# First x of a fused attention and MoE kernel by casting loads on GpSimd's queue, transposed head by head, with the first weight chunk in halves

## The chip, the cores and the metric

The kernel runs on one core of one Trainium2 chip. The metric is the device time of one execution in microseconds (us), lower is better. The core has five engines with programs of their own: PE (TensorE, matrix products; its weight loads are listed as PEld), DVE (VectorE), ACT (ScalarE), POOL (GpSimd) and SP (SyncE, here only a queue for transfers). They meet through semaphores. Sixteen DMA engines carry the transfers that SP, ACT and POOL issue.

## The reference

```python
# x: (B 8, H 8, S 512, D 64)   state: (8, 8, Ns 32, 64)   scale = 1/8
a      = softmax(scale * x @ state^T)          # (B,H,512,32)
xread  = a @ state                             # (B,H,512,64)
a2     = softmax(scale * state @ x^T)          # (B,H,32,512)
sread  = a2 @ x                                # (B,H,32,64)
t      = concat([xread, sread], axis=2)        # (B,H,544,64)
t      = t.transpose(0,2,1,3).reshape(4352, 512)
h      = t @ w_in                              # 512 -> 2048
out    = (h / (1 + exp(-h))) @ w_out           # silu, 2048 -> 512
```

Inputs and output are fp32; the kernel computes in bf16 with fp32 sums.

## The kernel before, in words

**Tiling.** The 512 features are four groups `kt` of 128 (two heads, `half` 0 and 1, of 64 each). The 512 rows of a batch are four groups `c` of 128, row 4p+c on partition p. The kernel goes batch by batch. `xread @ w_in` is not computed through xread: the state of a batch is first multiplied with w_in, and the result `W1` (`w1_m` on PE into two PSUM banks, `w1_e` to copy it out as bf16) has 256 rows (8 heads x 32 states), so that `h = a @ W1` (`g1`, two matmuls of 128x512 and a silu on ACT) and `out = g @ w_out` (`G2(b, ft)`: four matmuls, one for each row group `tt`; `ft` counts sixteen groups of 128 of the 2048 features).

**One batch's attention.** x arrives as fp32 (`load_x`), is cast to bf16 into `x_n` (`cast_x`; its rows have a column of ones on either side, for the sums of sread), transposed on PE (`x_T`, four 128x128 transposes for one kt) and copied out of PSUM into `xT` (`x_Te`). `st_T` transposes the state and writes the two halves of `sbd`. `sc` computes the scores of one kt (four matmuls), `ex` exponentiates them on ACT into `en`, `norm_s` sums and inverts on DVE, `norm_m` multiplies into `an`, and `a_T` transposes `an` on PE and copies it into `aT`, which g1 reads. `sread_m`, `sread_n` and `sread_t` compute sread from `en` and `x_n`.

**Order.** The order of instructions is written out by hand (`manual_schedule`): each engine executes its own in the order of the program. Transfers are in order within the issuing engine too: an engine that waits holds up the transfers written behind the wait. A load that POOL issues takes one of eight semaphores in turn, and the ninth waits until the first of them is done. For batch 0 (lines 327 to 412): SP issues four loads of x (one kt each, line 91), ACT issues the state (line 327), POOL builds the identity, casts the state, and issues the first w_in chunk (512 of 2048 columns), the first w_out chunk (four ft), the state of batch 1 and the second w_in chunk. All w loads cast fp32 to bf16 in the transfer. PE fills its idle time with `warm` matmuls on zeros (line 320). DVE casts x (line 79 is `cp` on DVE, line 83 `cp` on ACT, line 81 on POOL); the four kt go through transposes, copies, scores and exponentials one after the other; then come the two halves of the normalization (POOL takes kt 0 and 1, DVE kt 2 and 3, line 185), the first `w1_m` and `w1_e`, `a_T`, and the first g1. After that the g1 and G2 of batch 0 are interleaved with the attention of batch 1 and the later chunks of `W1` (lines 411 to 482). From batch 1 on, `phase(k, fill)` runs the 64 matmuls of batch k's G2 and inserts the attention and g1 of the next batches at numbered steps; x is there transposed by DMA.

Of the kernel before, what the change touches and what calls it, by code (L numbers as in the profile page):

```python
# [19 lines left out]
def kernel(  # L20
# [8 lines left out]
    nc = tc.nc  # L29
# [16 lines left out]
    x_f = [pers.tile([128, KT, 2, 256], FP32, name=f"x_f{i}") for i in range(2)]  # L46
    x_n = [pers.tile([128, KT, 4, 132], BF16, name=f"x_n{i}") for i in range(2)]
    x_u = pers.tile([128, KT, 4, 2, D], BF16, name="x_u")
    xT = [pers.tile([128, KT, 4, 128], BF16, name=f"xT{i}") for i in range(2)]
# [27 lines left out]
    def cp(eng, dst, src):  # L77
        if eng == "dve":
            nc.vector.tensor_copy(dst, src)  # L79
        elif eng == "pool":  # L80
            nc.gpsimd.tensor_copy(dst, src)
        else:
            nc.scalar.activation(dst, src, func=COPY, bias=0.0)  # L83
# [5 lines left out]
    def load_x(b, eng, kt=0, n=4):  # L89
        dst = x_f[b % 2][:, ds(kt, n)].rearrange("p k h e -> p (k h) e")  # L90
        eng.dma_start(dst, x_src(b, kt, n))
# [3 lines left out]

    def load_wi(j):
        nc.gpsimd.dma_start(
            w_in_sb[:, :, ds(512 * j, 512)], win_re[:, :, ds(512 * j, 512)]
        )

    def load_wo(j):
        nc.gpsimd.dma_start(w_out_sb[:, ds(4 * j, 4), :], wout_re[:, ds(4 * j, 4), :])

# [23 lines left out]
    def x_T(b, kt, bk):  # L127
        v = bf(bk).rearrange("p (k c t) -> p k c t", k=2, c=4)
        for c in range(4):
            nc.tensor.transpose(  # L130
                v[:, kt % 2, c, :], x_n[b % 2][:, kt, c, ds(2, 128)], ident[:]
            )

    def x_Te(b, kt, n, bk, eng):
# [111 lines left out]

    def w1_m(b, j, bks):
        for kt in range(KT):
            for half in range(2):
                nc.tensor.matmul(  # L250
                    bank[bks[half]][ds(32 * kt, 32), :],
                    sbd[ds(64 * half, 64), b, kt, half, :],
                    w_in_sb[ds(64 * half, 64), kt, ds(512 * j, 512)],
                    start=True,
                    stop=True,
                    skip_group_check=True,
                    tile_position=(64 * half, 32 * kt),
                )

    def w1_e(b, j, bks, engs):  # L260
        for half in range(2):
            cp(engs[half], W1[b % 2][:, half, ds(512 * j, 512)], bank[bks[half]][:])

# [61 lines left out]
    with tc.manual_schedule():  # L325

        nc.scalar.dma_start(st0_f[:], state[0].rearrange("h ns d -> ns h d"))
        for kt in range(KT):
            load_x(0, nc.sync, kt, 1)
        nc.vector.memset(zeros[:], 0.0)  # L330
        nc.vector.memset(sbd[:], 0.0)
        for i in range(2):
            nc.vector.memset(x_n[i][:, :, :, 1:131:129], 1.0)
        make_identity(nc, ident[:])
        nc.scalar.preload_act_table(EXP)
        cp("pool", st_nat[:, 0, :], st0_f[:])
        load_wi(0)
        load_wo(0)
        load_st(1)
        load_wi(1)  # L340
        warm(28, "o0")

# [12 lines left out]
        def W1x(b, j, bks, engs):  # L355
            w1_m(b, j, bks)
            w1_e(b, j, bks, engs)

# [13 lines left out]

        cast_x(0, "dve", (0,))
        x_T(0, 0, XB[0])
        x_Te(0, 0, 1, XB[0], "act")
        cast_x(0, "dve", (1,))
        st_T(0, "a1", "act", "dve")
        cast_x(0, "dve", (2, 3))
        warm(4, "w1")
        x_T(0, 1, XB[1])  # L380
        x_Te(0, 1, 1, XB[1], "act")
        sc(0, 0, SB[0])
        ex(0, 0, 1, SB[0])
        warm(3, "w1")
        x_T(0, 2, XB[2])
        x_Te(0, 2, 1, XB[2], "act")
        sc(0, 1, SB[1])
        ex(0, 1, 1, SB[1])
        x_T(0, 3, XB[3])
        x_Te(0, 3, 1, XB[3], "dve")  # L390
        warm(2, "o0")
        for kt in (2, 3):
            sc(0, kt, SB[kt])
            ex(0, kt, 1, SB[kt])
        norm_s(0, 0, 2)
        norm_m(0, "pool", 0, 2)
        norm_s(0, 2, 2)
        norm_m(0, "dve", 2, 2)
        nc.scalar.preload_act_table(SILU)
        warm(7, "o0", 512)  # L400
        w1_m(0, 0, ("w0", "w1"))
        w1_e(0, 0, ("w0", "w1"), ("act", "act"))
        a_T(0, (("a0", "dve"), ("a1", "dve")))
        warm(2, "o0", 512)
        load_x(1, nc.gpsimd, 0, 2)
        load_x(1, nc.gpsimd, 2, 2)
        load_wo(1)
        load_wi(2)


        for ft in range(4):
            g1(0, ft)
        G2(0, 0)
        st_T(1, "a0", "dve", "dve")
        sread_m(0, "a1")
        sread_n(0, "a1")
        G2(0, 1)
        sread_t(0, "a1", "dve")
        G2(0, 2)
        W1x(0, 1, AB, DA)  # L420
# [7 lines left out]
        cast_x(1, "dve", (2,))  # L428
        load_wo(2)
        load_wi(3)  # L430
        load_wo(3)
        load_x(2, nc.gpsimd)
# [54 lines left out]
        def W1p(b, i):  # L487
            for j in range(2):
                w1_m(b, 2 * i + j, WP[j])
            for j in range(2):  # L490
                w1_e(b, 2 * i + j, WP[j], DD if j == 0 else ("act", "act"))

# [103 lines left out]
```

## Time and profile before

| | us |
|---|---|
| median of 13 runs | 223.31 |
| lowest and highest | 222.42, 226.24 |
| the profiled execution | 222.59 |
| its span (first to last instruction) | 220.8 |
| PE busy in the span | 210.2 |
| ACT busy | 133.3 |
| DVE busy | 83.6 |
| POOL busy | 40.7 |
| first g1 matmul starts | 11.77 |

How to read the profile's rows: a row of the timeline has the start, the time that the group covers, the engine and line of the code, the operation, what it writes and reads, how many instructions are merged in it, and in brackets how long the engine had been idle before, with what ended that. L79 is line 79. "x4" are four instructions. A window row has the busy time of each engine in that stretch with the instructions in brackets, then the granted clock, the mean busy share of the 16 DMA engines (over 1 where transfers overlap in an engine) and the GB/s that were written. "DMA to landing" counts from the start of the issuing instruction to the transfer's end. The loads of before that matter here: x from SP is issued at 0.74, 1.27, 1.76 and 2.29 us and lands after 2.6, 3.3, 3.5 and 3.7 us; the first w_in chunk is issued at 4.13 and lands after 5.5; the first w_out chunk at 5.06, after 7.7; the second w_in chunk at 6.49, after 9.0; the second w_out chunk at 11.67, after 10.3, and G2(0, 4), which reads it, starts at 22.01.

### The profile page before, as it was taken

What the parts mean: (1) busy time and instruction counts of PE and PEld (TensorE: products, weight loads), DVE (VectorE), ACT (ScalarE), POOL (GpSimd) and SP (SyncE); (2) the same over time, 40 slices, a digit from 0 to 9 for tenths busy, and PEclk for the clock granted to TensorE, in tenths of its full rate; (3) what the DMA queues carried; (4) which work ended last, traced back from release to release, by engine and by line L of the source; (5) the groups of instructions that cost most, each with busy time, mean ns of one, the idle gap of its engine ahead of it and who ended that gap; (6) DMA issues with size and microseconds to landing.
All of it is one profiled execution on the core that took longest, in us unless ns stands there. A gap on an engine that the chain in (4) does not pass through costs nothing.

```text
span 220.8 us, 4060 instructions
## 1 busy us (share of the span) xinstructions
PE 210.2 (95%) x1626; PEld 102.9 (47%) x1654; DVE 83.6 (38%) x162; ACT 133.3 (60%) x220; POOL 40.7 (18%) x78
## 2 busy tenths in 40 slices
PE   7799999999999999999999999999999999999993
PEld 7444433445444444444444444444453444566552
DVE  4736253526840483138412851085206701111110
ACT  3845876586568946776477837692669377433210
POOL 4634722005200052002500250025000200000000
PEclk9999999999999999999999999999999999999999
DMA  6999997292070386118540655066511311111112
GB/s 202 152 264 234 182 268 90 79 269 84 3 190 0 81 240 160 47 39 223 157 107 0 216 169 120 25 186 194 99 47 47 98 47 47 53 47 47 47 50 95
DMA packets 33988, 26.00 MB, mean 118 GB/s; under 512 B 18736, under 2 KB 29232, under 8 KB 33968
## 3 DMA queue, kind: packets, MB, share of 16 engines
q1 hardware_dynamic: 26720, 18.75, 30.2%
q0 software_dynamic: 6688, 6.52, 16.4%
q10 hardware_dynamic: 560, 0.46, 0.6%
q8 instruction: 13, 0.21, 0.4%
q14 instruction: 7, 0.06, 0.1%
HBM read 17.30 MB, written 8.91 MB: 119 GB/s over the span
## 4 chain that ended last, share of the span: by engine, by line
PE 87%; ACT 4%; DMA 3%; issue 3%; POOL 1%; DVE 1%; ACTq 0%
PE ps_o L295 44%; PE ps_h L271 25%; PE ps_w L295 4%; PE ps_h L282 3%; DMA aT<-an 3%; PE ps_o L320 2%; PE ps_a L159 2%; PE ps_w L250 2%; POOL an L185 1%; PE ps_a L250 1%; PE ps_h L250 1%; ACT W L83 1%; PE ps_a L217 1%; PE ps_a L130 1%; ACT g L279 1%
## 5 line engine op out<-in xcount | busy, mean ns | idle before, releaser
L295 PE MATMUL ps_o<-w_out_sb,g 128*128 128x512 bf16 x458 | 126.5, 379 | 2.5 <-issue 1.9
L279 ACT ACTIVATE g<-ps_h 128x512 bf16<-128x512 f32 x128 | 75.5, 598 | 51.0 <-PE ps_h L271 49.3
L271 PE MATMUL ps_h<-aT,W 128*128 128x512 bf16 x251 | 74.0, 379 | 1.1 <-ACT g L279 0.6
L295 PEld LDWEIGHTS <-g 128*128 128x128 bf16 x512 | 47.9, 98 | 52.5 <-issue 3.9
L79 DVE COPY o_sb<-ps_o 128x512 f32<-128x512 f32 x30 | 20.6, 689 | 90.7 <-PE ps_o L295 69.6
L271 PEld LDWEIGHTS <-W 128*128 128x128 bf16 x256 | 24.2, 98 | 32.1 <-DMA aT<-an 2.7
L185 POOL TENSOR_TENSOR an<-en,rs 128x512 bf16<-128x512 bf16 x7 | 10.0, 1429 | 90.6 <-ACT W L83 49.7
L141 POOL CAST x_u<-x_f 128x256 bf16<-128x256 f32 x40 | 14.2, 406 | 24.0 <-DMA x_f<-in_x_dram 24.0
L79 DVE CAST W<-ps_w 128x512 bf16<-128x512 f32 x24 | 15.4, 682 | 0.4 <-PE ps_w L250 0.3
L83 ACT ACTIVATE W<-ps_h 128x512 bf16<-128x512 f32 x24 | 13.1, 602 | 0.5 <-PE ps_h L250 0.5
L290 ACT ACTIVATE g_s<-ps_h 128x256 bf16<-128x256 f32 x16 | 6.1, 384 | 11.4 <-PE ps_h L282 11.4
L180 DVE TENSOR_REDUCE rs<-en 128x32 f32<-128x1024 bf16 (+1 forms) x9 | 9.8, 1094 | 4.1 <-ACT en L170 4.1
L170 ACT ACT_TABLE_LOAD x7 | 9.0, 1283 | 1.8 <-DVE xT L79 1.6
L282 PE MATMUL ps_h<-xsT,w_in_sb 128*128 128x256 bf16 x64 | 9.6, 273 | 0.0
L295 PE MATMUL ps_w<-w_out_sb,g 128*128 128x512 bf16 x32 | 9.5, 379 | 0.1
L170 ACT ACTIVATE en<-ps_a 128x512 bf16<-128x512 f32 (+1 forms) x16 | 8.3, 568 | 0.2
L282 PEld LDWEIGHTS <-w_in_sb 128*128 128x128 bf16 x64 | 6.3, 98 | 4.1
L506 ACT ACT_TABLE_LOAD x6 | 7.7, 1283 | 0.1
L159 PEld LDWEIGHTS <-xT 128*128 128x128 bf16 x128 | 5.9, 98 | 3.6 <-ACT xT L83 0.3
L79 DVE COPY sbd<-ps_a 64x128 bf16<-64x128 bf16 x15 | 4.3, 289 | 8.6 <-PE ps_a L119 8.2
L79 DVE CAST W<-ps_a 128x512 bf16<-128x512 f32 x6 | 4.2, 692 | 9.0 <-PE ps_a L250 9.0
L250 PEld LDWEIGHTS <-sbd 64*32 64x32 bf16 x256 | 3.1, 89 | 9.0 <-issue 8.8
(61 smaller groups left out, 129.2 us busy)
## 6 DMA issues: line engine op xcount, KB each, us to landing
out_dram<-o_sb SPq DMA_DIRECT2D x32, 256.0 KB, 2.5
x_f<-in_x_dram SPq DMA_DIRECT2D x5, 1024.0 KB, 7.0
w_in_sb<-in_moe_w_in_dram POOLq DMA_DIRECT2D x4, 512.0 KB, 8.9
w_out_sb<-in_moe_w_out_dram POOLq DMA_DIRECT2D x4, 512.0 KB, 9.0
x_f<-in_x_dram SPq DMA_DIRECT2D x4, 256.0 KB, 3.4
x_f<-in_x_dram POOLq DMA_DIRECT2D x2, 512.0 KB, 8.4
x_f<-in_x_dram POOLq DMA_DIRECT2D x1, 1024.0 KB, 12.8
out_dram<-o_sb ACTq DMA_DIRECT2D x1, 256.0 KB, 2.5
```

The costliest lines, as they stand in the source:

```text
L79: nc.vector.tensor_copy(dst, src)
L83: nc.scalar.activation(dst, src, func=COPY, bias=0.0)
L141: nc.gpsimd.tensor_copy(x_u[:, kt, :, h, :], x_f[b % 2][:, kt, h, :].rearrange("p (c d) -> p c d", c=4),)
L159: nc.tensor.matmul(v[:, kt % 2, :, c, :], xT[b % 2][:, kt, c, :], sbd[:, b, kt, :, :], start=True, stop=True, skip_group_check=True,)
L170: nc.scalar.activation(en[b % 2][:, :, :, ds(kt, n), :].rearrange("p h c k s -> p k (h c) s"), v[:, ds(kt % 2, n)], func=EXP, bias=0.0, sc ...
L180: nc.vector.tensor_reduce(v, en[b % 2][:, :, :, ds(kt, n), :], axis=AX, op=ADD)
L185: e.tensor_tensor(an[b % 2][:, :, :, ds(kt, n), :].rearrange("p h c k s -> p (h c) k s"), en[b % 2][:, :, :, ds(kt, n), :].rearrange("p h ...
L250: nc.tensor.matmul(bank[bks[half]][ds(32 * kt, 32), :], sbd[ds(64 * half, 64), b, kt, half, :], w_in_sb[ds(64 * half, 64), kt, ds(512 * j, ...
L271: nc.tensor.matmul(bk[:], W1[b % 2][:, half, ds(128 * ft, 128)], aT[b % 2][:, half, :, :], start=(half == 0), stop=(half == 1), skip_group ...
L279: nc.scalar.activation(g[b % 2][:, ft, :], bk[:], func=SILU, bias=0.0)
L282: nc.tensor.matmul(bk[:, 0:256], w_in_sb[:, kt, ds(128 * ft, 128)], xsT[:, kt, :, :, :], start=(kt == 0), stop=(kt == KT - 1), skip_group_ ...
L295: nc.tensor.matmul(bank[bk][:, c0:c1], src[:, ft, ds(128 * tt, 128)], w_out_sb[:, ft, c0:c1], start=(ft == 0), stop=(ft == 15), skip_group ...
```

## The change

- x of batch 0 no longer goes through `x_f` and DVE casts. POOL's queue loads it as bf16, cast in the transfer, into a new tile `x_0` that is ordered by head: kt 0, kt 1, then kt 2 and 3 together. The loads are the first thing that POOL does; the identity is built after them. The state of batch 0 is loaded from SP and cast on DVE.
- `x_T0` transposes `x_0` head by head: eight transposes of 128 rows x 64 columns for one kt, into the upper or lower half of the partitions. `pad_x0` copies `x_0` into the padded `x_n` later, in four DVE copies behind the first g1.
- The first w_in chunk and the first w_out chunk are loaded in two halves each, in turns. `w1_m` and `w1_e` take a first column and a width; batch 0's first 512 columns are made in two steps of 256, the second of them between the second g1 and the first G2. The second w_in chunk is issued after POOL's `norm_m`.
- Order: the first half of the normalization is put ahead of the transposes of kt 2 and 3; `st_T` leaves both copies to DVE; xT of kt 1 is copied by DVE; the second copy of aT goes to ACT; g1 and G2 alternate at the beginning; the counts of warm matmuls are 26, 3, 5 and 1 in place of 28, 4, 3, 2, 7 and 2.

```diff
--- before.py
+++ after.py
@@ -45,6 +45,7 @@
     sbd = pers.tile([128, B, KT, 2, NS], BF16, name="sbd")
     x_f = [pers.tile([128, KT, 2, 256], FP32, name=f"x_f{i}") for i in range(2)]
     x_n = [pers.tile([128, KT, 4, 132], BF16, name=f"x_n{i}") for i in range(2)]
+    x_0 = pers.tile([128, KT, 2, 4, D], BF16, name="x_0")
     x_u = pers.tile([128, KT, 4, 2, D], BF16, name="x_u")
     xT = [pers.tile([128, KT, 4, 128], BF16, name=f"xT{i}") for i in range(2)]
     en = [pers.tile([128, 2, 4, KT, NS], BF16, name=f"en{i}") for i in range(2)]
@@ -93,13 +94,16 @@
     def gate(b):
         nc.vector.memset(x_f[b % 2][ds(0, 1), 0, 0, ds(0, 1)], 0.0)
 
-    def load_wi(j):
+    def load_wi(c0, n):
+        nc.gpsimd.dma_start(w_in_sb[:, :, ds(c0, n)], win_re[:, :, ds(c0, n)])
+
+    def load_wo(f0, n):
+        nc.gpsimd.dma_start(w_out_sb[:, ds(f0, n), :], wout_re[:, ds(f0, n), :])
+
+    def load_x0(kt, n):
         nc.gpsimd.dma_start(
-            w_in_sb[:, :, ds(512 * j, 512)], win_re[:, :, ds(512 * j, 512)]
-        )
-
-    def load_wo(j):
-        nc.gpsimd.dma_start(w_out_sb[:, ds(4 * j, 4), :], wout_re[:, ds(4 * j, 4), :])
+            x_0[:, ds(kt, n)].rearrange("p k h c d -> p (k h) (c d)"), x_src(0, kt, n)
+        )
 
     def load_st(b):
         nc.gpsimd.dma_start(st_nat[:, b, :], state[b].rearrange("h ns d -> ns h d"))
@@ -130,6 +134,21 @@
             nc.tensor.transpose(
                 v[:, kt % 2, c, :], x_n[b % 2][:, kt, c, ds(2, 128)], ident[:]
             )
+
+    def x_T0(kt, bk):
+        v = bf(bk).rearrange("p (k c t) -> p k c t", k=2, c=4)
+        for c in range(4):
+            for half in range(2):
+                nc.tensor.transpose(
+                    v[ds(64 * half, 64), kt % 2, c, :], x_0[:, kt, half, c, :], ident[:]
+                )
+
+    def pad_x0(kt, eng):
+        cp(
+            eng,
+            x_n[0][:, kt, :, ds(2, 128)].rearrange("p c (h d) -> p h c d", h=2),
+            x_0[:, kt],
+        )
 
     def x_Te(b, kt, n, bk, eng):
         v = bf(bk).rearrange("p (k c t) -> p k c t", k=2, c=4)
@@ -244,22 +263,22 @@
         )
 
 
-    def w1_m(b, j, bks):
+    def w1_m(b, c0, n, bks):
         for kt in range(KT):
             for half in range(2):
                 nc.tensor.matmul(
-                    bank[bks[half]][ds(32 * kt, 32), :],
+                    bank[bks[half]][ds(32 * kt, 32), 0:n],
                     sbd[ds(64 * half, 64), b, kt, half, :],
-                    w_in_sb[ds(64 * half, 64), kt, ds(512 * j, 512)],
+                    w_in_sb[ds(64 * half, 64), kt, ds(c0, n)],
                     start=True,
                     stop=True,
                     skip_group_check=True,
                     tile_position=(64 * half, 32 * kt),
                 )
 
-    def w1_e(b, j, bks, engs):
+    def w1_e(b, c0, n, bks, engs):
         for half in range(2):
-            cp(engs[half], W1[b % 2][:, half, ds(512 * j, 512)], bank[bks[half]][:])
+            cp(engs[half], W1[b % 2][:, half, ds(c0, n)], bank[bks[half]][:, 0:n])
 
     hctr = [0]
 
@@ -324,21 +343,22 @@
 
     with tc.manual_schedule():
 
-        nc.scalar.dma_start(st0_f[:], state[0].rearrange("h ns d -> ns h d"))
-        for kt in range(KT):
-            load_x(0, nc.sync, kt, 1)
+        nc.sync.dma_start(st0_f[:], state[0].rearrange("h ns d -> ns h d"))
+        load_x0(0, 1)
+        load_x0(1, 1)
+        load_x0(2, 2)
+        make_identity(nc, ident[:])
+        load_wi(0, 256)
+        load_wo(0, 2)
+        load_wi(256, 256)
+        load_wo(2, 2)
+        load_st(1)
         nc.vector.memset(zeros[:], 0.0)
         nc.vector.memset(sbd[:], 0.0)
         for i in range(2):
             nc.vector.memset(x_n[i][:, :, :, 1:131:129], 1.0)
-        make_identity(nc, ident[:])
         nc.scalar.preload_act_table(EXP)
-        cp("pool", st_nat[:, 0, :], st0_f[:])
-        load_wi(0)
-        load_wo(0)
-        load_st(1)
-        load_wi(1)
-        warm(28, "o0")
+        warm(26, "o0")
 
         XB = ("o0", "o1", "w0", "w1")
         SB = ("h0", "h1", "a0", "a1")
@@ -353,8 +373,8 @@
                 g2(b, tt, ft, OB[tt])
 
         def W1x(b, j, bks, engs):
-            w1_m(b, j, bks)
-            w1_e(b, j, bks, engs)
+            w1_m(b, 512 * j, 512, bks)
+            w1_e(b, 512 * j, 512, bks, engs)
 
         def exs(b):
             ex(b, 0, 2, "a0")
@@ -370,53 +390,56 @@
                 sc(b, kt, AB[q])
 
 
-        cast_x(0, "dve", (0,))
-        x_T(0, 0, XB[0])
+        cp("dve", st_nat[:, 0, :], st0_f[:])
+        x_T0(0, XB[0])
         x_Te(0, 0, 1, XB[0], "act")
-        cast_x(0, "dve", (1,))
-        st_T(0, "a1", "act", "dve")
-        cast_x(0, "dve", (2, 3))
-        warm(4, "w1")
-        x_T(0, 1, XB[1])
-        x_Te(0, 1, 1, XB[1], "act")
+        st_T(0, "a1", "dve", "dve")
+        x_T0(1, XB[1])
+        x_Te(0, 1, 1, XB[1], "dve")
         sc(0, 0, SB[0])
         ex(0, 0, 1, SB[0])
         warm(3, "w1")
-        x_T(0, 2, XB[2])
-        x_Te(0, 2, 1, XB[2], "act")
         sc(0, 1, SB[1])
         ex(0, 1, 1, SB[1])
-        x_T(0, 3, XB[3])
+        norm_s(0, 0, 2)
+        norm_m(0, "pool", 0, 2)
+        x_T0(2, XB[2])
+        x_Te(0, 2, 1, XB[2], "act")
+        x_T0(3, XB[3])
         x_Te(0, 3, 1, XB[3], "dve")
-        warm(2, "o0")
         for kt in (2, 3):
             sc(0, kt, SB[kt])
             ex(0, kt, 1, SB[kt])
-        norm_s(0, 0, 2)
-        norm_m(0, "pool", 0, 2)
         norm_s(0, 2, 2)
         norm_m(0, "dve", 2, 2)
         nc.scalar.preload_act_table(SILU)
-        warm(7, "o0", 512)
-        w1_m(0, 0, ("w0", "w1"))
-        w1_e(0, 0, ("w0", "w1"), ("act", "act"))
-        a_T(0, (("a0", "dve"), ("a1", "dve")))
-        warm(2, "o0", 512)
+        w1_m(0, 0, 256, ("w0", "w1"))
+        w1_e(0, 0, 256, ("w0", "w1"), ("act", "act"))
+        warm(5, "o0", 512)
+        a_T(0, (("a0", "dve"), ("a1", "act")))
+        warm(1, "o0", 512)
+        load_wi(512, 512)
         load_x(1, nc.gpsimd, 0, 2)
         load_x(1, nc.gpsimd, 2, 2)
-        load_wo(1)
-        load_wi(2)
-
-
-        for ft in range(4):
-            g1(0, ft)
+        load_wo(4, 4)
+        load_wi(1024, 512)
+
+
+        g1(0, 0)
+        g1(0, 1)
+        w1_m(0, 256, 256, AB)
+        w1_e(0, 256, 256, AB, DA)
+        for kt in range(KT):
+            pad_x0(kt, "dve")
         G2(0, 0)
+        g1(0, 2)
+        G2(0, 1)
+        g1(0, 3)
         st_T(1, "a0", "dve", "dve")
         sread_m(0, "a1")
         sread_n(0, "a1")
-        G2(0, 1)
+        G2(0, 2)
         sread_t(0, "a1", "dve")
-        G2(0, 2)
         W1x(0, 1, AB, DA)
         G2(0, 3)
         g1(0, 4)
@@ -426,9 +449,9 @@
         W1x(1, 0, AB, DA)
         g1(0, 6)
         cast_x(1, "dve", (2,))
-        load_wo(2)
-        load_wi(3)
-        load_wo(3)
+        load_wo(8, 4)
+        load_wi(1536, 512)
+        load_wo(12, 4)
         load_x(2, nc.gpsimd)
         for b in range(2, B):
             load_st(b)
@@ -486,9 +509,9 @@
 
         def W1p(b, i):
             for j in range(2):
-                w1_m(b, 2 * i + j, WP[j])
+                w1_m(b, 1024 * i + 512 * j, 512, WP[j])
             for j in range(2):
-                w1_e(b, 2 * i + j, WP[j], DD if j == 0 else ("act", "act"))
+                w1_e(b, 1024 * i + 512 * j, 512, WP[j], DD if j == 0 else ("act", "act"))
 
         def phase(k, fill):
             for tt in range(4):
```

## The prediction

> **What bounds the kernel now.** I read the page first: its busy table and the chain that ended last.
>
> ```profile
> span 220.8 us, 4060 instructions
> ...
> PE 210.2 (95%) x1626; PEld 102.9 (47%) x1654; DVE 83.6 (38%) x162; ACT 133.3 (60%) x220; POOL 40.7 (18%) x78
> ...
> PE 87%; ACT 4%; DMA 3%; issue 3%; POOL 1%; DVE 1%; ACTq 0%
> ```
>
> The end is set by TensorE. From the first g1 on (11.77 us) it streams: the list of waits names for it none above 0.5 us there, so what the change does to the first 11 us moves the end one for one, unless a load holds the stream up later. The second view is the timeline of that start:
>
> ```profile
> 3.34 0.49 DVE L79 CAST x_n<-x_f 128x256 bf16<-128x256 f32 x2 [0.92 <-DMA x_f<-in_x_dram]
> ...
> 4.13 0.94 POOL L97 DMA_DIRECT2D w_in_sb<-in_moe_w_in_dram  x1
> 4.15 0.63 PE L130 MATMUL ps_o<-ident,x_n 128*128 128x128 bf16 x4
> ...
> 7.48 0.42 DVE L79 COPY xT<-ps_w 128x512 bf16<-128x512 bf16 x1 [0.49 <-PE ps_w L130]
> 7.57 0.38 ACT L170 ACTIVATE en<-ps_h 128x256 bf16<-128x256 f32 x1
> ...
> 7.99 0.69 DVE L180 TENSOR_REDUCE rs<-en 128x16 f32<-128x512 bf16 x1
> 8.06 0.66 ACT L170 ACTIVATE en<-ps_a 128x256 bf16<-128x256 f32 x2
> ...
> 8.71 0.25 DVE L181 RECIPROCAL rs<-rs 128x16 f32<-128x16 f32 x1
> ...
> 8.88 0.63 DVE L180 TENSOR_REDUCE rs<-en 128x16 f32<-128x512 bf16 x1
> 9.12 1.05 POOL L185 TENSOR_TENSOR an<-en,rs 128x512 bf16<-128x512 bf16 x1 [1.83 <-DVE rs L181]
> ...
> 9.82 0.90 DVE L185 TENSOR_TENSOR an<-en,rs 128x512 bf16<-128x512 bf16 x1
> ...
> 10.87 0.61 PE L201 MATMUL ps_a<-ident,an 128*128 128x128 bf16 x8 [0.75 <-ACT W L83]
> ...
> 11.29 0.76 DVE L79 COPY aT<-ps_a 128x512 bf16<-128x512 bf16 x2 [0.57 <-PE ps_a L201]
> ```
>
> The reader is to see a chain: last xT copy (ends 7.90), scores, last exp (ends 8.72), row sum, reciprocal, product (ends 10.72), a_T (10.87), aT copies, g1. The row at 10.87 names ACT, but the second DVE product ends 0.15 us before it; that is what it waits for. I call 10.87 the mark A. The third view is the busy time by windows of 1 us, for the transfers:
>
> ```profile
> 6.00:7.00 1.00, 0.75 (x15) 0.58 (x14) 0.99 (x4) 0.81 (x2) 1.00 (x2) 1.00 0.53 80
> 7.00:8.00 1.00, 0.82 (x16) 0.59 (x14) 0.44 (x2) 0.87 (x2) 0.29 (x1) 1.00 1.22 197
> ```
>
> The last column is GB/s written, the one before it the DMA share: the engines are full at about 200 GB/s of bf16, so 400 GB/s of fp32 read.
>
> **What the skill says.** (1) "DMA: Bandwidth & Descriptors", section "SWDGE vs HWDGE vs iDMA": a DMA that casts has to be issued from GpSimd, and its "Specifications" put the first byte at about 1 us there, against 0.6 us from SP. The trace agrees in direction: x from SP is issued at 0.74 and lands after 2.6 us; the first w_in load, 1.05 MB read, is issued at 4.13 and lands after 5.5 us, of which 0.524 MB at 200 GB/s is 2.6, so 2.9 us of start-up. (2) The same page, "Issuing engines are not separate DMA queues": loads from all queues share 16 engines. The trace agrees: share above 1 from 7 us on, with POOL's queue alone. (3) "TensorE: Matmul & The Clock Gate", Part 1: TensorE runs at half rate until a free-running window of about 3.4 us was busy; Part 4 adds that transposes don't count as busy in the same way. The trace shows the warm matmuls 107 ns apart and the ones after 5.6 us 56 ns apart; that transposes count less no run here shows.
>
> **The change part by part.**
>
> *x by casting loads.* POOL's first own instruction stands at 0.73; the x loads go there. Issue of the first costs 0.94 (as the w_in row), then 0.75 each: done at 3.2, identity (0.21+0.29 and gaps) at 3.75. Start-up is not shown for an empty queue at time 0: between SP's 1.7 us (2.6 less 0.26 MB at 300 GB/s) and POOL's 2.9. I take 2.9, the same queue. Data: 0.26 MB at 400 GB/s is 0.65 us per kt. Landings: 0.73+2.9+0.65 = 4.3, 4.9, and 6.2 for the last pair, where before had 3.34 and 5.98. The eight DVE casts go, but the first transposes start at 4.3 where they started at 4.15.
>
> *Eight transposes instead of four.* Each has 128 columns still, so at 107 ns: 0.86 us for kt 0 (4.3 to 5.15), state transpose to 5.26, kt 1 by 5.86 (three at 107, five at 56 ns). If the two halves ran side by side, half of that; I take none.
>
> *DVE takes over.* DVE now does both sbd copies (0.59, from 5.5 to 6.1) and the xT copy of kt 1 (0.42, to 6.53). Then by the rows' gaps (0.06 copy to scores, 0.33 scores to exp): scores 6.59, exp 6.92 to 7.30. The first row sum and reciprocal (0.69+0.25) now stand ahead of the last xT copy on DVE: 7.33 to 8.30. Queued behind them is that copy, and behind it scores, exp and the whole second half. kt 2 and 3 are transposed from 6.8 to 7.7 (landed at 6.2), so their data would be ready at 7.92, and the copy waits 0.4 us for DVE: 8.33 to 8.75, against 7.90 before. Scores 8.81, last exp 9.14 to 9.52, against 8.72: **+0.8**.
>
> *After the exp.* Row sum 0.63, reciprocal 0.25, product. The product took 0.90 beside POOL's (9.12 to 10.17); POOL's now runs before it, and the same shape took 0.69 elsewhere (row at 56.8 us): I take 0.75. A at 11.43: **+0.56**.
>
> *First weights in halves.* w_in, w_out, w_in, w_out of 0.52 MB each are issued from 3.75 to 6.8 and follow x without the gap that the window 6 to 7 shows. First half lands at about 7.7, needed at 8.9: nothing. The later ones (9.0, 10.3, 11.6) are needed from A+2 = 13.4: nothing. The ACT copies of half a chunk (0.38 each) run from 10.8, after the table load (1.28), and end by 11.6, before ACT's aT copy is due at 12.1. wi(512,512) is now issued after POOL's product, at 9.4, when the queue still has 2 us of data: no hole, and w_out 1, which landed at 11.67+10.3 = 21.97 for a use at 22.01, comes at the same time or up to 0.5 earlier.
>
> *From A to the second chunk.* Before: DVE's two aT copies end at A+1.2, four g1 with a wait of 0.4 for the g copies, G2(0,0) from A+3.2, two G2 done at A+4.96. After: the second aT copy on ACT (0.60 where DVE takes 0.42) ends at A+1.3; two g1; w1_m of 256 columns costs 0.34 in the stream (0.45 for 512 columns by the rows at 17 us, less 0.11); G2(0,0) at A+2.4 after silu; g1, G2, g1: done at A+5.0. What the split adds fills the wait that it takes away: **0**. The four pads on DVE (an estimate from 0.69 for four times the elements: 0.2 each) end at A+4, before sread at A+5.4; if they were late, TensorE would stop there by the difference.
>
> Sum: +0.6 on the profiled execution's 222.59 (span 220.8 and 1.8 around it), that is 223.2. That execution is among the quickest of the 13; on the median 223.31 it is **223.9**.
>
> **Rivals.**
> - *Side by side and quick.* POOL's start-up is 1.7 us and the two halves of a transpose overlap: kt 1's copy ends at 5.9, everything after it 0.6 earlier: +0.0, 223.3. For it: nothing else holds DVE. Against: the 2.9 us measured on this queue.
> - *The clock comes up late* (the slower one). Place: 4 to 6 us, where 26 warm matmuls end at 3.97 and, with the four at 4.68 gone, transposes alone follow. If those don't count, TensorE stays at 107 ns. Price: kt 2 and 3 take 1.7 instead of 0.9 (+0.8 at the exp), the five wide warm matmuls at 430 ns hold a_T up by 0.2, a_T and the first g1 at half rate cost 0.8: +1.8 in place of 0, with the rest 225.7 at most, 225.2 if it comes up midway. It decides if the clock is still half at 6.5 us. For it: the spread of the runs before, 222.42 to 226.24, looks like a start that is not always the same.
> - *Slow x packets.* The casting x load writes 512 B pieces, half of the weights' 1 KB. If each piece costs as much as a weight's, x takes 5.2 us, the last pair lands at 8.8 and A moves by 2.1 to 13.5: 226.
> - *The loads absorb it.* Had A come earlier, w_out 1 at 21.97 would stop G2(0,4): no gain above 0.5 can reach the end. It caps a gain and adds nothing to a loss.
>
> **How the numbers follow.** Forecast 223.9 (own range 223.2 to 224.5): 0.48. Quick: 0.17. Late clock: 0.22. Slow packets: 0.13. A measurement of this kernel tells about 0.5% (1.1 us) from no change, so 222.2 to 224.4 is "same". Late clock and slow packets are slower, with a twentieth of the forecast; quick gives about 0.08 for faster. Faster 0.08, same 0.54, slower 0.38. The range 222.6 to 226.0 leaves out a tenth on each side.
>
> **What would show it.** In the profile after: first x transposes near 4.3, the 56 ns spacing from about 5.6, DVE's row sum ahead of the last xT copy and that copy near 8.3, last exp ending near 9.5, a_T near 11.4, and from there to 220 us the same distance as before (span 221.4). Wrong would be: x transposes before 3.8, a copy of kt 3 that doesn't wait for DVE, matmuls 107 ns apart after 6.5, or a wait on w_in or w_out in the stream.

## The result, and the profile after

| | before | after |
|---|---|---|
| median, both on the same chip (us) | 223.48 (48 runs) | 225.86 (11 runs) |
| lowest and highest | 222.16, 226.67 | 224.61, 228.0 |
| ratio after to before | | 1.0104, interval 1.0075 to 1.0133 |
| the profiled execution | 222.59 | 225.49 |
| its span | 220.8 | 223.7 |

The change makes the kernel slower by 1.0%, 2.4 us in the medians and 2.9 us between the two profiled executions. The time lies inside the range of the prediction, 0.14 us below its upper end; the single number was 2.0 us too low. The page of the kernel after:

```profile
span 223.7 us, 4080 instructions
...
PE 211.9 (95%) x1639; PEld 103.8 (46%) x1667; DVE 83.3 (37%) x161; ACT 133.3 (60%) x220; POOL 44.0 (20%) x82
...
PE 74%; issue 9%; DMA 9%; POOL 3%; ACT 2%; DVE 1%; POOLq 1%; SPq 0%
```

TensorE is busy for 1.7 us more, part of it warm matmuls at half rate. In the chain that ended last, DMA had 3% and has 9%, and POOL had 1% and has 3%: the chain now begins in x's load on POOL's queue. The timeline of the start of the kernel after:

```profile
1.25 2.38 POOL L104 DMA_DIRECT2D x<-in_x_dram  x3 [0.80 <-POOLq L603]
...
4.16 0.76 POOL L98 DMA_DIRECT2D w_in_sb<-in_moe_w_in_dram  x1
...
4.59 0.64 PE L142 MATMUL ps_o<-ident,x 128*64 128x128 bf16 x8 [0.44 <-DMA x<-in_x_dram]
...
7.43 1.06 PE L142 MATMUL ps_w<-ident,x 128*64 128x128 bf16 x16 [0.40 <-DMA x<-in_x_dram]
7.49 0.69 DVE L199 TENSOR_REDUCE rs<-en 128x16 f32<-128x512 bf16 x1 [0.96 <-ACT en L189]
...
8.54 0.42 DVE L80 COPY xT<-ps_w 128x512 bf16<-128x512 bf16 x1
...
9.20 0.66 ACT L189 ACTIVATE en<-ps_a 128x256 bf16<-128x256 f32 x2 [0.49 <-PE ps_a L178]
...
9.90 0.42 PE L269 MATMUL ps_w<-w_in_sb,sbd 64*32 64x256 bf16 x8 [0.49 <-DMA w_in_sb<-in_moe_w_in_dram]
...
10.65 1.91 PE L339 MATMUL ps_o<-zeros 128*128 128x512 bf16 x4 [0.33 <-issue]
...
10.90 0.69 DVE L204 TENSOR_TENSOR an<-en,rs 128x512 bf16<-128x512 bf16 x1
...
12.36 1.06 PE L220 MATMUL ps_a<-ident,an 128*128 128x128 bf16 x8
...
13.57 0.38 PE L290 MATMUL ps_h<-aT,W 128*128 128x512 bf16 x1
...
19.36 0.39 PE L269 MATMUL ps_a<-w_in_sb,sbd 64*32 64x512 bf16 x1
19.47 0.44 DVE L80 COPY xsT<-ps_a 128x128 bf16<-128x128 bf16 x1 [0.32 <-PE ps_a L258]
19.96 0.41 PE L269 MATMUL ps_a<-w_in_sb,sbd 64*32 64x512 bf16 x7 [0.22 <-DVE xsT L80]
```

Read against the rows of before, from the top. POOL issues x at 1.25, and x lands 3.3, 3.2 and 4.5 us after its issue, at 4.55, 5.33 and 7.39; before, SP's loads landed from 3.3 to 6.0. Eight transposes take 0.64 us at half rate, sixteen take 1.06. The last exp ends at 9.86 (before 8.72). The first half of w_in, issued at 4.16, lands at 9.86, and W1 waits for it. Behind W1 stand wide warm matmuls at half rate, 427 ns apart, and they hold `a_T` until 12.36, although the product that it needs is there at 11.59. In before, such matmuls ran ahead of W1, at full rate:

```profile
8.30 1.46 PE L320 MATMUL ps_o<-zeros 128*128 128x512 bf16 x6
...
9.71 0.41 PE L250 MATMUL ps_w<-w_in_sb,sbd 64*32 64x512 bf16 x8
```

The first g1 of the kernel after starts at 13.57 (11.77). At 19.36 one W1 matmul runs and the other seven wait until DVE has copied xsT. The windows from 6 to 8 us of the kernel after, to be set beside those of before (last columns: DMA share, GB/s written):

```profile
6.00:7.00 1.00, 0.89 (x13) 0.75 (x11) 0.50 (x2) 0.38 (x1) 1.00 (x2) 1.00 1.39 155
7.00:8.00 1.00, 0.60 (x13) 0.57 (x14) 0.51 (x1) 0.38 (x1) 0.77 (x2) 1.00 1.35 158
```

The engines now have no gap here, but 155 to 158 GB/s where the weights alone came at 197: x and the first halves of the weights, all of one queue, are in flight together.

Three marks cut the span. A is the start of `a_T`. M is the start of the last matmul of a W1 group further down the stream, ahead of a wait of 0.4 us for ACT that both kernels have. The third is the end.

| profiled execution | A | A to M | M to end | span |
|---|---|---|---|---|
| before | 10.87 | 16.94 | 192.99 | 220.8 |
| after | 12.36 | 17.85 | 193.49 | 223.7 |
| difference | +1.49 | +0.91 | +0.50 | +2.9 |

So the question was what of the start costs 2.4, and whether the last 0.5 belongs to the change.

### The profile page after: what moved, and what is told of

Read it like the earlier page. It is cut to its first block, busy times and chain, and to the rows that moved or that the text cites. A ratio compares the mean times of both kernels' runs of the same rounds, so it can differ in the third digit from the quotient of the medians.

```text
span 223.7 us, 4080 instructions
## 1 busy us (share of the span) xinstructions
PE 211.9 (95%) x1639; PEld 103.8 (46%) x1667; DVE 83.3 (37%) x161; ACT 133.3 (60%) x220; POOL 44.0 (20%) x82
## 4 chain that ended last, share of the span: by engine, by line
PE 74%; issue 9%; DMA 9%; POOL 3%; ACT 2%; DVE 1%; POOLq 1%; SPq 0%
PE ps_o L314 37%; PE ps_h L290 21%; DMA aT<-an 4%; PE ps_w L314 4%; PE ps_h L301 3%; DMA w_in_sb<-in_moe_w_in_dram 3%; DMA x_f<-in_x_dram 2%; PE ps_w L269 1%; PE ps_a L178 1%; PE ps_a L269 1%; POOL x L104 1%; POOL x_u L160 1%; PE ps_h L269 1%; PE ps_o L339 1%; PE ps_a L236 1%
## 5 line engine op out<-in xcount | busy, mean ns | idle before, releaser
L80 DVE CAST W<-ps_a 128x512 bf16<-128x512 f32 (+1 forms) x7 | 4.6, 654 | 10.0 <-PE ps_a L269 10.0
## 6 DMA issues: line engine op xcount, KB each, us to landing
x_f<-in_x_dram POOLq DMA_DIRECT2D x1, 1024.0 KB, 13.5
```

## The experiments

Four causes were tried. **Queue**: x on POOL's queue comes later, and the weights behind it too. **Clock**: TensorE is at half rate until about 13.5 us because fewer warm matmuls run. **Order**: W1 of the second chunk now stands directly behind `sread_t`. **Fetch**: TensorE has 26 instructions more, its instruction blocks arrive at other places of the program, and there they delay a transfer that PE waits for. Each median stands beside the runs of the kernel before on the same chip (223.16 for the first eight kernels, 223.57 for the last four).

### Warm matmuls kept in the kernel after

```diff
-        warm(26, "o0")
+        warm(34, "o0")
...
         st_T(0, "a1", "dve", "dve")
+        warm(4, "w1")
```

> The changed kernel with TensorE kept busy early: 34 warm matmuls instead of 26 ahead of the first x transposes, and the four warm matmuls of before back between the state transpose and the transposes of kt 1. Theory CLOCK (the profile of the changed kernel has half rate until 13.7 us, where before had it until 5.6, since transposes alone follow the warm matmuls): full rate by about 6 to 7 us, 1.2 to 1.7 us faster than the changed kernel, so 224.1 to 224.6, about 0.9 over before. Theory LOADS (x and w_in land later, the chain hangs on them and the rate matters little): within 0.3 us of the changed kernel, or slower by the 0.4 us of added matmuls. Theory ORDER (the sread transpose just ahead of the W1 matmuls): within 0.3 us.

Measured: 227.92 us, ratio 1.0184 (1.0131 to 1.0237), slower than the changed kernel. The clock did come up early. The timeline of this kernel:

```profile
8.33 0.64 PE L142 MATMUL ps_w<-ident,x 128*64 128x128 bf16 x16 [1.66 <-DMA x<-in_x_dram]
...
9.77 0.66 ACT L189 ACTIVATE en<-ps_a 128x256 bf16<-128x256 f32 x2 [0.38 <-PE ps_a L178]
...
12.31 0.61 PE L220 MATMUL ps_a<-ident,an 128*128 128x128 bf16 x8 [0.68 <-DVE an L204]
```

Sixteen transposes take 0.64 in place of 1.06, but they start 0.9 later, because PE waits 1.66 us for x, whose last pair landed at 8.29 here and at 7.39 in the kernel after. The last exp ends 0.57 later (10.43). From there the full clock wins time: 1.88 us to A, where `a_T` now waits for DVE, in place of 2.50, and 17.40 from A to M in place of 17.85. Together that is 1.1 us, of which the late x takes 0.57 back: M is at 29.71, 0.5 ahead of the kernel after. The time shows no gain: M to the end is 2.3 us longer than in the kernel after, with 2.7 us of waits for aT (see the fetch experiments). So this run does not clear the clock of a part in the loss, and the median does not confirm one.

### Fewer warm matmuls in the kernel before

```diff
-        warm(28, "o0")
+        warm(26, "o0")
...
-        warm(4, "w1")
```

> The kernel before with 26 warm matmuls instead of 28 and without the four warm matmuls behind the state transpose, as the change has it; nothing else. Theory CLOCK: half rate until 9 us or later, 1 to 2 us slower than before (224.5 to 225.5). Theory LOADS or ORDER: the same as before within 0.3 us.

Measured: 223.77 us, ratio 1.0014 (0.9986 to 1.0042). Here the clock reached full rate only at 10.2 us (5.65 before), and A moved from 10.87 to 11.25, M by 0.3. In the kernel before a late clock alone is worth 0.3 us at M, and 0.3 us in the time, give or take 0.6: not the whole loss. There the wide warm matmuls stand ahead of W1, so this does not price a late clock in the order of the changed kernel.

### The state matmuls of batch 1 as before, in the kernel after

```diff
-        G2(0, 1)
         g1(0, 3)
         st_T(1, "a0", "dve", "dve")
         sread_m(0, "a1")
         sread_n(0, "a1")
-        G2(0, 2)
+        G2(0, 1)
         sread_t(0, "a1", "dve")
+        G2(0, 2)
         W1x(0, 1, AB, DA)
```

> The changed kernel with G2(0,1) moved from ahead of the fourth g1 to behind sread_n, so that, as before, a G2 stands between the sread transpose and the W1 matmuls that write the same PSUM bank. Theory ORDER: the wait of W1 on the xsT copy goes, 0.5 to 0.6 us faster than the changed kernel (225.3). Theories CLOCK and LOADS: no difference over 0.2 us.

Measured: 226.07 us, ratio 1.0101 (1.0054 to 1.0148). The timeline of this kernel at the same place:

```profile
18.48 0.44 DVE L80 COPY xsT<-ps_a 128x128 bf16<-128x128 bf16 x1 [0.33 <-PE ps_a L258]
18.71 0.59 PE L314 MATMUL ps_w<-w_out_sb,g 128*128 128x512 bf16 x2
19.23 0.41 PE L269 MATMUL ps_a<-w_in_sb,sbd 64*32 64x512 bf16 x8
```

The copy runs under G2, and all eight W1 matmuls go in one piece, as in before:

```profile
17.39 0.41 PE L250 MATMUL ps_a<-w_in_sb,sbd 64*32 64x512 bf16 x8
```

A to M is 16.88, as before (16.94); the changed kernel has 17.85. Only a part of this 0.97 is the order: `a_T` takes 0.67 here, since the clock came up just then, and 1.06 in the kernel after. Where `a_T` runs at full rate, the new order takes 17.40 (kept-busy kernel above, x from SP below) and the old one 16.84 to 17.00 (seven kernels). So the order costs about 0.5 us between A and M, and half rate about 0.45. Yet the median did not move, and the profiled execution of this kernel has a wait of 1.16 us for aT, up to 155.6 us, that gives it back. This was the reason to look at the middle of the kernel.

### Only x by casting loads, in the kernel before

```diff
-        for kt in range(KT):
-            load_x(0, nc.sync, kt, 1)
+        load_x0(0, 1)
+        load_x0(1, 1)
+        load_x0(2, 2)
...
-        cast_x(0, "dve", (0,))
-        x_T(0, 0, XB[0])
+        x_T0(0, XB[0])
```

> The kernel before with one part of the change alone: x of batch 0 by casting loads on GpSimd's queue, first in it, transposed head by head, padded into x_n behind the first four g1; the weight loads, the warm matmuls, the engines and the order as before. Theory LOADS: last pair of x lands at about 7.4 us instead of 6.0 and the first w_in chunk 1 us later: 1.0 to 1.6 us slower than before. Theory CLOCK: warm matmuls are as before, full rate by 6 to 7 us, so at most 0.5 us slower.

Measured: 225.88 us, ratio 1.0100 (1.0067 to 1.0133): the whole loss, with one part of the change (and the transposes head by head and the pads that go with it). The timeline of this kernel:

```profile
7.89 0.64 PE L144 MATMUL ps_w<-ident,x 128*64 128x128 bf16 x8 [0.70 <-DMA x<-in_x_dram]
...
10.16 3.17 PE L341 MATMUL ps_o<-zeros 128*128 128x512 bf16 x7
...
13.27 0.48 PE L271 MATMUL ps_w<-w_in_sb,sbd 64*32 64x512 bf16 x8
13.68 0.62 PE L222 MATMUL ps_a<-ident,an 128*128 128x128 bf16 x8
```

The last x lands at 7.85, and A is 13.68: here seven wide warm matmuls at half rate take 3.17 us and stand in front of W1 and `a_T`. They were written to fill a gap, and they fill more than the gap when they run at half rate.

### x of the kernel after from SP again

x is loaded as fp32 from SP and cast on DVE into `x_0`; the state comes through ACT's queue and is cast on POOL.

```diff
-        load_x0(0, 1)
-        load_x0(1, 1)
-        load_x0(2, 2)
+        for kt in range(KT):
+            load_x(0, nc.sync, kt, 1)
...
+        cast_x0(0)
         x_T0(0, XB[0])
```

> The changed kernel with the load path of x undone: x as fp32 from SP, the state from ACT, both cast on chip (x by DVE into the same tile x_0, four casts of 128x512; the state by POOL ahead of the weight loads); head-by-head transposes, halves of the weights, order and warm matmuls as changed. Theory LOADS (the late landing of x and, behind it, of w_in is the cost): last kt of x lands at 6.0, first half of w_in by 8, a_T by 11.0 to 11.5; 1.3 to 1.8 us faster than the changed kernel, 224.2, what is left being the sread order (0.6). Theory CLOCK (few warm matmuls): still half rate beyond 9 us, at most 0.5 faster than the changed kernel.

Measured: 225.35 us, ratio 1.0077 (1.0050 to 1.0105). x landed at 3.79, 4.73, 5.49 and 6.16, A came at 11.26, M at 28.66 in place of 30.21. The median gained 0.6 us on the ratios, with an interval of 0.9 to either side: the mark says 1.5, the end does not say so. This profiled execution too has a wait for aT, of 1.0 us up to 154.4. And it is not a typical one. Five of the 22 executions, this one among them, have a mean granted clock of 0.992 (here half from 7.6 to 11.0 us, then full) and take 223.54 to 224.31 us; the other 17 take 224.61 to 226.88. So with x early the clock of the start goes with some 1.8 us between the two groups' medians. The groups were made afterwards, and whether the clock is the cause was not tried.

### Plain x loads on POOL's queue, in the kernel before

```diff
-            load_x(0, nc.sync, kt, 1)
+            load_x(0, nc.gpsimd, kt, 1)
```

> The kernel before with its four plain fp32 loads of x issued by POOL instead of SP, first in that queue; nothing else. Theory QUEUE (the start-up of GpSimd's queue, issue at 1.25 and 3.3 us to the first landing, makes x late): first x at 4.5, last near 6.8, 0.8 to 1.5 us slower than before. Theory PIECES (the cast into pieces of 512 bytes makes x late): the plain loads follow as fast as SP's, last x at 6.0 to 6.3, within 0.5 us of before.

Measured: 225.49 us, ratio 1.0103 (1.0078 to 1.0128), with one word changed. The timeline of this kernel:

```profile
1.26 3.06 POOL L91 DMA_DIRECT2D x_f<-in_x_dram  x4 [0.82 <-POOLq L580]
...
4.75 1.48 DVE L79 CAST x_n<-x_f 128x256 bf16<-128x256 f32 x4 [2.32 <-DMA x_f<-in_x_dram]
...
7.31 1.13 DVE L79 CAST x_n<-x_f 128x256 bf16<-128x256 f32 x4 [0.39 <-DMA x_f<-in_x_dram]
...
12.64 0.41 PE L250 MATMUL ps_w<-w_in_sb,sbd 64*32 64x512 bf16 x8 [0.43 <-DMA w_in_sb<-in_moe_w_in_dram]
12.99 0.62 PE L201 MATMUL ps_a<-ident,an 128*128 128x128 bf16 x8
```

x lands at 4.73, 5.45, 7.29 and 7.93 without any cast in the transfer, and the first w_in chunk, for which W1 and `a_T` wait, at 12.60 in place of 9.67. The same loss comes without the cast and its small pieces: it is the queue that x is in.

### The first chunk whole, in the kernel after

```diff
-        load_wi(0, 256)
-        load_wo(0, 2)
-        load_wi(256, 256)
-        load_wo(2, 2)
+        load_wi(0, 512)
+        load_wo(0, 4)
...
-        w1_m(0, 256, 256, AB)
-        w1_e(0, 256, 256, AB, DA)
```

> The changed kernel with the halves undone: first w_in chunk of 512 columns in one load, first w_out chunk of four ft in one load, W1 of 512 columns in one step ahead of the five wide warm matmuls. Theory HALVES HELP (with x late in the same queue, the first half is what lets W1 start at 9.9): the whole chunk lands near 11.3, W1 and the warm matmuls behind it hold a_T up by about 1 us, 0.7 to 1.2 us slower than the changed kernel. Theory HALVES COST (smaller pieces and one more W1 step): 0.3 us faster.

Measured: 229.82 us, ratio 1.0255 (1.0214 to 1.0296). In its timeline W1 waits for the whole chunk, and `a_T` comes at 13.29:

```profile
11.17 0.41 PE L269 MATMUL ps_w<-w_in_sb,sbd 64*32 64x512 bf16 x8 [1.62 <-DMA w_in_sb<-in_moe_w_in_dram]
```

With x ahead of the weights the halves win 1.3 us at M, and more than that at the end (2.0 us of it a wait for aT in this profile). Here they repair a part of what x in the same queue costs; with x in another queue the whole chunk was not tried against them.

### g1 of the middle phases later, in the kernel before

```diff
-            att_tail(fill, k + 1, 0, 24, 33, 1.9)
+            att_tail(fill, k + 1, 0, 24, 37, 1.7)
```

The g1 blocks of phases 2 to 6, which read the aT that the transfer brings, become due later, and so get slack against its landing.

> The kernel before with the g1 of the next batch inserted later in phases 2 to 6 (from step 37 in strides of 1.7 in place of 33 in strides of 1.9), so that the transfer that transposes aT has about 1 us more before its first reader; nothing else. Theory SPREAD (the scatter of all kernels here, 4 us from run to run, comes from this transfer landing after 3.1 to 4.8 us, for which TensorE waits in single phases): lowest time unchanged at 222.2 to 222.6, median 0.5 to 0.9 lower, scatter about halved. If the scatter has its cause in the first 14 us (clock, x): no difference.

Measured: 222.58 us, ratio 0.9950 (0.9926 to 0.9974): quicker than both kernels. Its profiled execution had a late w_in (12.30) and M at 29.53, and still ended with a span of 222.3, because from M to the end it took 192.8. Nothing of its start is edited, and before had w_in at 9.67 and M at 27.81: the marks of one execution can move by 1.7 us by themselves. They tell where the time goes; how much a change costs is told by the medians.

### The fetch theory

aT of the later batches is made by a DMA transpose that SP issues, and the g1 that reads it has hardly any slack against its landing. In all 14 profiled executions there are 70 such transfers. 57 land 3.0 to 3.3 us after the issue, and 13 after 3.5 to 5.0. In 12 of the 13, a block of 16 KB of TensorE's instructions (a queue of its own, 13 blocks in each run) arrived 0.4 to 2.8 us after the issue; of the other 57 transfers one had such a block at that place. The thirteenth, in a kernel below, had a block of another engine's instructions 0.34 us after the issue; at 0.2 to 0.8 us such a block did nothing in eight others, so this one stays unexplained. The same stretch of before and after, seen by DMA queue from just after the issue (queue and kind: packets, MB, share; then the transfers issued, with us from issue to landing):

```profile
q1 hardware_dynamic: 1317, 0.61, 84.9%
issues: line engine op xcount, KB each, median us to landing
...
aT<-an SPq DMA_TRANSPOSE x1, 3.3
```

```profile
q1 hardware_dynamic: 1164, 0.37, 73.8%
q8 instruction: 1, 0.02, 2.0%
issues: line engine op xcount, KB each, median us to landing
...
aT<-an SPq DMA_TRANSPOSE x1, 3.5
```

The first is before (issue at 149.38, no block inside), the second is after (issue at 151.78, a block at 152.38). Where the blocks fall depends on how many instructions TensorE has had: that is why a kernel with 26 more of them can lose in a place that nobody edited. Two kernels test it: 26 instructions added to before, and 26 taken from after.

```diff
         w1_e(0, 0, ("w0", "w1"), ("act", "act"))
+        warm(13, "o0", 8)
```

> The kernel before with 13 small matmuls of 8 columns (26 rows on TensorE's queue, some 0.5 us in a gap where TensorE waits for the product anyway), so that its later instruction blocks come as many rows earlier as in the changed kernel. Theory A (block fetches): the block that arrived at 153.80, after the last-but-one aT transfer (issued 149.38), now falls inside it, that transfer takes over 3.4 us in place of 3.3, and the time rises by 0.5 to 1.5 us to about 223.7 to 224.7. Theory B (the start alone): no change, 223.2 within 0.5, and the aT transfers land after 3.1 to 3.3 us.

Measured: 224.3 us, ratio 1.0017 (0.9981 to 1.0053). Its waits, then the DMA queues of the stretch behind the issue at 149.33:

```profile
PE ps_h L271 <- DMA aT<-an: 1.2, 2, 1.0
```

```profile
q1 hardware_dynamic: 710, 0.30, 86.5%
q8 instruction: 1, 0.02, 2.0%
issues: line engine op xcount, KB each, median us to landing
...
aT<-an SPq DMA_TRANSPOSE x1, 4.1
```

The mechanism came as foretold: the block, now at 150.61, lies inside the transfer, which takes 4.1 us where it took 3.3, and PE waits 1.0. The median does not tell it from no change: 0.4 us more on the ratios, between 0.4 less and 1.2 more.

```diff
-        warm(26, "o0")
+        warm(13, "o0", 256)
```

> The changed kernel with its first 26 warm matmuls of 128 columns as 13 of 256: the same columns and the same time, 26 rows fewer on TensorE's queue, as many as in the kernel before. Theory A (block fetches): the block at 152.38 moves out of the aT transfer issued at 151.78, which lands after 3.1 us again, and the time falls by 0.5 to 1.5 us to 224.4 to 225.4. Theory B (the start alone): the same as the changed kernel, 225.9 within 0.5.

Measured: 226.61 us, ratio 1.0126 (1.0093 to 1.0159): not quicker than the kernel after. The transfer at 154.84 landed after 3.1 us, as foretold, but two others came late. The timeline of this kernel, at the two g1 concerned:

```profile
106.08 1.24 SPq L226 DMA_TRANSPOSE aT<-an  x1
...
110.47 0.60 PE L290 MATMUL ps_h<-aT,W 128*128 128x512 bf16 x2 [1.28 <-DMA aT<-an]
...
130.51 1.24 SPq L226 DMA_TRANSPOSE aT<-an  x1
...
134.80 0.61 PE L290 MATMUL ps_h<-aT,W 128*128 128x512 bf16 x2 [1.18 <-DMA aT<-an]
```

A block of TensorE's came 1.5 us behind the first issue. So late transfers make single executions hard to compare, by about 1 us each time. Moving the blocks did not undo the slowdown, but it did not take the waits away either; the next kernel does.

### The later g1 in the kernel after

```diff
-            att_tail(fill, k + 1, 0, 24, 33, 1.9)
+            att_tail(fill, k + 1, 0, 24, 37, 1.7)
```

> The changed kernel with the g1 blocks of phases 2 to 6 due later (37 and 1.7 for 33 and 1.9 in att_tail's arguments), which gave the kernel before 222.6. Both theories: the waits for aT in the middle go, and what the start costs stays. Theory A: a gain over the changed kernel of about 1.0 to 1.6 us, more than the 0.6 to 1.1 that it gave before, so 224.3 to 224.9. Theory B: a gain as before, 0.6 to 1.1, so 224.8 to 225.3. Against the same edit in the kernel before it stays 1.7 to 2.4 us slower under both: that is the start.

Measured: 225.53 us, ratio 1.0078 (1.0054 to 1.0102). In its list of waits no matmul waits for aT any more (one weight load does, 0.6 us, as in before with the later g1), though one transfer took 4.0 us: the slack took it. From M (30.34) to the end it takes 192.96, the same as before (192.99). The gain of 0.3 us (0.6 on the ratios) is no more than the same edit gave in before, which speaks for the start as the cause. Against the same edit in before (0.9950) the changed kernel stays 1.3% slower (2.9 us, give or take 0.8, the two intervals taken as independent). Neither of the two has a matmul that waits for aT, so fetch is not the cause of the 2.4 us.

### x from SP, the old order and the later g1, in the kernel after

The edits of three kernels above together; the chief lines:

```diff
-        load_x0(0, 1)
-        load_x0(1, 1)
-        load_x0(2, 2)
+        for kt in range(KT):
+            load_x(0, nc.sync, kt, 1)
...
-        G2(0, 2)
+        G2(0, 1)
         sread_t(0, "a1", "dve")
+        G2(0, 2)
...
-            att_tail(fill, k + 1, 0, 24, 33, 1.9)
+            att_tail(fill, k + 1, 0, 24, 37, 1.7)
```

> The changed kernel with x as plain FP32 loads from SyncE's queue and casts on VectorE, G2(0,1) moved behind the state matmuls, and the g1 blocks of phases 2 to 6 due later: each suspect of the slowdown undone, the head-by-head transposes and the halves of the first chunk kept. If the causes are these three, it comes to the time of the kernel before with the later g1, 222.6 within 0.5; if the transposes head by head, the halves or the new order cost something of their own, it stays above 223.3.

Measured: 223.54 us, ratio 1.0019 (0.9995 to 1.0043). That is 0.6%, give or take 0.3%, under the kernel just above (1.3 us on the ratios) and 0.7%, give or take 0.3%, above the kernel before with the later g1 (1.5 us on the ratios): the mended version is no better than before, and something of the change beside the queue and the order still costs. Its timeline shows where:

```profile
7.00 1.06 PE L142 MATMUL ps_w<-ident,x 128*64 128x128 bf16 x16
...
7.52 0.69 DVE L202 TENSOR_REDUCE rs<-en 128x16 f32<-128x512 bf16 x1 [0.23 <-ACT en L192]
...
8.41 0.36 DVE L80 COPY xT<-ps_w 128x512 bf16<-128x512 bf16 x1
...
8.77 0.87 ACT L192 ACTIVATE en<-ps_a 128x256 bf16<-128x256 f32 x2 [0.49 <-PE ps_a L181]
```

The transposes end at 8.06, but DVE does the row sum and the reciprocal first, and copies xT only at 8.41; the last exp ends at 9.64, 0.9 behind before (8.72), and M is 28.79, 1.0 behind. That is the very step of DVE that the prediction priced. How the rest of it is shared between DVE's casts of whole kts, the half rate (the sixteen transposes take 1.06 here, 0.64 at full rate) and the second aT copy on ACT was not tried apart.

## Why the prediction was right or wrong

The range held with 0.14 us to spare, because room had been left for two slower rivals; the sum itself gave +0.6 where +2.4 came, so that the range held is luck in good part. The view that TensorE's stream hands a delay of the start on to the end did hold: M to the end is 192.99 before and 192.96 in the changed kernel with the later g1. The likeliest case, 223.9, did not come. Step by step:

- **x by casting loads: mis-sized.** It put the landings at 4.3, 4.9 and 6.2; they were 4.55, 5.33 and 7.39. POOL's first issue came at 1.25, not at 0.73, where in before POOL's first memset stood; and the second half of x took 2.1 us behind kt 1, where 400 GB/s of fp32 would have made 1.3. The plain loads on the same queue show the same delay, so the term that failed is the queue's start and pace, not the cast. "DMA: Bandwidth & Descriptors" of the Trainium skill, section "Latency and other measured facts", puts the first byte of the two kinds of queue only 0.4 us apart; the first x landed 3.3 us after its issue here and 2.6 from SP in before, 0.7 apart, and with the later issue 1.2 us later in all.
- **Eight transposes, none side by side: wrong, and cheap.** They ran in pairs: eight in 0.64 us at half rate, where four of the 128x128 kind took 0.63 in before. "TensorE: Matmul & The Clock Gate" of the skill, "Part 3: Packing small matmuls", says that matmuls on different tiles of the array overlap, and the trace agrees. But the chain waited for x and then for DVE, not for the transposes, so being quicker brought nothing.
- **DVE's row sum ahead of the last xT copy: right in place, hidden in the event.** The copy was put at 8.33 to 8.75 and ran from 8.54 to 8.96. But the transposes ended at 8.49 and the reciprocal at 8.46: x was late by as much as DVE. With x from SP, in the last kernel, the wait of 0.35 for DVE stands free. The exp was put at 9.52 and ended at 9.86.
- **After the exp: right.** 1.76 us to the product's end were forecast, 1.73 it took.
- **"First half lands at about 7.7, needed at 8.9: nothing": the step that failed most at A.** It landed at 9.86: x ahead of it was late, and from 4 to 9 us all loads of the queue together moved 155 to 170 GB/s. W1 began at 9.90, the wide warm matmuls behind it at 10.65, four of them at half rate until 12.36. So `a_T` started 0.77 after its product in place of 0.15. Together with the 0.3 of the exp this makes A +1.49 where +0.56 was forecast. The whole-chunk kernel shows that halves were worth 1.3 us at M, not nothing: the slack that the prediction saw at W1 was not there, and that hid a gain and a loss at once.
- **"From A to the second chunk: 0": failed by 0.9.** Four g1 and two G2 were done 5.41 us after A (4.93 before, the state matmuls between them left out), with `a_T` at half rate (1.06 for 0.61) and the second aT copy on ACT; and W1 behind `sread_t` waited 0.6 for xsT. The forecast walked the stream only up to two G2 and did not see that without a G2 between them W1 writes the PSUM bank a1 while DVE still has to read `sread_t` from it. The old order at full rate takes 16.88, as before; the new order at full rate takes 17.40.
- **The weights of later chunks: right.** No wait on w_in or w_out after the first shows in the list.

Of the rivals, the late clock was the nearest in its number (225.2 to 225.7), and by its own test, half rate after 6.5 us, it came. The profiled execution splits the 2.4 us at M so: the product is 0.87 late, behind x and DVE; the wide warm matmuls at half rate hold `a_T` for 0.62 more, which the rival had priced at 0.2; `a_T` and what follows at half rate make some 0.45, priced at 0.8; the order makes some 0.5. So about 1.1 of it falls in steps at half rate, the 0.62 only because W1 was late as well. What the clock costs in the time is not shown: alone in before it was 0.3 us, and curing it in the changed kernel gave no gain, with x later in that profile. Slow packets came in half the size (7.39, not 8.8) and by another cause, as plain loads are as slow. Side by side was true, quick was not. That loads absorb a gain was not tested, as there was none.

What is shown: x on POOL's queue costs the kernel before 1.0% by itself; the old order gives about 0.5 us back between A and M; mending both takes off 0.6% where the middle has slack. What stays open: the share of each, and of the late clock, in the end of the changed kernel, since x from SP alone gave 0.6 us, give or take 0.9, and single medians here move by the aT waits too; and the split of the last 0.7%.

## What to carry to other kernels

Price a move between queues by the whole queue: when the first issue comes, what lands behind it, and which filler work on the waiting engine then sits in front of the late step. Halve what now stands behind the moved load, and follow a reordered block to the next writer of its PSUM bank, not only to the end of its own stage. When a trace shows a loss far from every edit, look for what shifted in place (here instruction blocks over a transfer without slack) and give that transfer slack: later g1 gained 0.5% in before, more than any version of the change.

## What the runs showed of the hardware

- A block of TensorE's instructions that arrives inside a DMA transpose goes with a landing after 3.5 to 5.0 us in place of 3.0 to 3.3 (12 of 13 such blocks between 0.4 and 2.8 us after the issue). "Runtime: NRT & Kernel Launch" of the skill, "Instruction fetch mechanics", has the blocks of 16 KB, which the trace confirms (13 of them, 0.21 MB), and calls their cost mostly hidden; in this kernel it was not, where the next reader had no slack. How the block delays the transfer was not tried.
- The first load on POOL's queue was issued at 1.25 us and on SP's and ACT's at 0.74. In the eight profiles with x on POOL's queue its first part landed at 4.5 to 5.0 us and its last at 7.3 to 8.3; in the six with x on SP's queue at 3.3 to 3.8 and 6.0 to 6.8.
- TensorE reached its full rate first between 4.0 and 13.5 us over the 14 profiles, and in five of them it fell to half rate again near the start, for 3.4 or 6.8 us. There the granted clock in the windows reads 0.50 (later g1 in the changed kernel, 8 to 13 us). Ahead of the first rise it reads 1.00 while matmuls of 128 columns stand 107 ns apart: there only their spacing shows the half rate.
